# Joining layer 1 and layer 3 tiles on one load of the A weights

## The chip, the cores and the metric

The kernel runs on one core of one Trainium2 chip. The metric is the device time of one execution in microseconds (us); the median of 12 runs of the kernel before is 2137.83 us (2132.86 to 2146.22). A core has a matrix engine (TensorE, PE in the profile; its weight loads are PEld), VectorE (DVE), ScalarE (ACT), GpSimd (POOL) and SyncE (SP), which here only issues transfers. Matmul results go to PSUM[...]; all other tiles lie in SBUF.

## The reference, cut to what matters

Four layers run over a sequence of 2048 positions with 576 features, each with a layernorm ahead of it and a residual sum behind it: A, B, A, B.

```python
x = A_x
x = x + _A_ref(_layernorm(x), A_wqkv, A_wo)                       # layer 1
x = x + _B_ref(_layernorm(x), B_mem0, B_Wq, B_Wk, B_Wv, B_Wo, 32) # layer 2
x = x + _A_ref(_layernorm(x), A_wqkv, A_wo)                       # layer 3
x = x + _B_ref(_layernorm(x), B_mem0, B_Wq, B_Wk, B_Wv, B_Wo, 32) # layer 4
```

A is a local attention: 32 heads of 18 features; each position attends to itself and to seven earlier positions, two apart, so a tile needs 14 positions (a halo) of the tile ahead of it. Its weights are `wqkv` (576 by 1728) and `wo` (576 by 576), and layers 1 and 3 use the same ones. B goes through the sequence in 64 segments of 32 positions, with 32 heads of 128 features and eight memory rows; the memory rows that come out of one segment go into the next, so B is a chain of 64 steps in each layer.

## The kernel before, in words

Activations are kept transposed, features on the partitions (576 = 4 x 128 + 64, so five chunks) and positions in the columns. A works on tiles of T = 64 positions (32 tiles in a layer), B on segments of 32.

**B** is done for layers 2 and 4 at once: in step t, lane 0 is segment t of layer 2 and lane 1 is segment t - 5 of layer 4 (`DLY` = 5), 69 steps in all. One step (`b_step`) has eleven groups of Q and K projections (`qk`, lines 832 and 835, 80 moving columns for both lanes), the V projections (`vpass`, line 879), two halves of scores and softmax (lines 919 to 929, then DVE, ACT, POOL), two halves of weighted sums (`pv`, line 970) and the output projection (`oproj`, line 994). Its weights stay in SBUF.

**A** is done by `a_tile(layer, j, ...)`, once for each of 64 (layer, tile) pairs. It does the layernorm (two PE sums at line 470, `stats` on DVE, `rstd` on ACT, `wr` on POOL), then Q, K and V: for each of the three parts, five output blocks `c` of 128 features, each the sum of five matmuls with 64 moving columns (line 570), then an evacuation `ev` for the part. The blocks start at the features `CB` = 0, 126, 252, 378, 448, so that no head is cut. Then come the products q times k on POOL, the logits on PE (line 619), a softmax, the spreading of the weights (line 644), the products with v on DVE, three adds, and the output projection (line 680, five blocks of five matmuls of 64 columns), the residual sum (line 686) and a second layernorm whose result, `xnb1` or `xnb3`, is B's input.

A's weights do not stay in SBUF. `wload` brings them in strips of up to 256 output features (`[128, 5*256]`, 320 KB, or 160 KB for a strip of 128): three strips for each of Q, K, V and three for the output, twelve for a tile. The very first tile takes them into the room of B's output weights; the next two gather them from the inputs (lines 503 and 504) into a ring of three buffers (`ring`), and the third writes each strip out to a contiguous copy (line 513); from then on they are fetched from that copy (line 507). Each load sits on SP's queue and waits until a ring buffer comes free. Layer 3's tile j is started when lane 0 has finished segments 2j and 2j+1; layer 1's tile j five steps ahead of its use (`LEAD`).

**The order of the work** is written out ahead of the run by a planner (`_Plan.run`). Every operation has a cost, a priority, the buffers that it takes and those that it gives back; the planner goes through time and gives each engine its next ready operation. What comes out is one fixed list of instructions for each engine, which the chip executes in that order. The planner has a cost for changing the matmul form (`SWITCH`, 0.097 us; forms F, C and R), and a model of PE's instructions arriving in pages of 256 (`PAGE`, `FETCH`). The dictionary `PR` holds the priorities.

Of the kernel before, what the change touches and what calls it, by code (L numbers as in the profile page):

```python
# [34 lines left out]
HPC = 7  # L35
EPS = 1e-5
NQ = T // 16
CB = (0, 126, 252, 378, 448)
# [202 lines left out]
def _evac(n):  # L241
    return (_act(n), _dve(n))
# [4 lines left out]

class _K:
    def __init__(self, ctx, tc, A_x, A_wqkv, A_wo, B_mem0, B_Wq, B_Wk, B_Wv, B_Wo, out):
        self.ctx, self.tc, self.nc = ctx, tc, tc.nc  # L250
        self.A_x, self.A_wqkv, self.A_wo = A_x, A_wqkv, A_wo
        self.B_mem0, self.B_Wq, self.B_Wk, self.B_Wv, self.B_Wo = B_mem0, B_Wq, B_Wk, B_Wv, B_Wo
        self.out = out
        _, self.S, d = A_x.shape
        assert d == D and self.S % P == 0
        assert B_Wq.shape[1] == NH and B_Wq.shape[2] == P and B_mem0.shape[1] == NM
        self.NT = self.S // T
        self.NSEG = self.S // SEG
        self.dly = DLY
        self.nsteps = self.NSEG + self.dly  # L260
        self.scale_b = float(P) ** -0.5
        self.pl = _Plan()
        self.halo = {}
# [22 lines left out]
    def setup(self):  # L286
# [8 lines left out]
        self.strips = [dp.tile([P, 5 * 256], BF16, name=f"strip{i}") for i in range(12)]  # L295
# [11 lines left out]
        for t_, pat, b0 in ((epad[:, 0:4, :], [[CB[1], 4]], 0), (epad[:, 4, :], [], CB[4])):  # L307
            self.sel(t_, pat + [[-AD, AH]], 1, b0, ALU.is_ge, 0.0)
            self.sel(t_, [[-a, n] for a, n in pat] + [[AD, AH]], -1, AD - 1 - b0, ALU.is_ge, 0.0)
        self.sel(epad[:, 0:4, :], [[0, 4], [0, AH]], -1, HPC * AD - 1, ALU.is_ge, 0.0)  # L310
        self.sel(epad[:, 4, :], [[0, AH]], 1, CB[4] - 4 * HPC * AD, ALU.is_ge, 0.0)
# [3 lines left out]
        for t_, pat, b0 in ((et[:, 0:4, :], [[CB[1], 4]], 0), (et[:, 4, :], [], CB[4])):  # L315
            self.sel(t_, pat + [[1, P]], -AD, b0, ALU.is_ge, 0.0)
            self.sel(t_, [[-a, n] for a, n in pat] + [[-1, P]], AD, AD - 1 - b0, ALU.is_ge, 0.0)
        nc.gpsimd.memset(et[:, 0:4, HPC * AD:P], 0.0)
        nc.gpsimd.memset(et[:, 4, 0:4 * HPC * AD - CB[4]], 0.0)
# [36 lines left out]
        tiles("qk", 7, [P, 3, 2, W80])  # L356
# [3 lines left out]
        tiles("x1", 2, [P, 5, T], F32)  # L360
        tiles("x3", 2, [P, 5, T], F32)
# [4 lines left out]
        tiles("xn", 1, [P, 5, T])  # L366
        tiles("qT", 1, [P, 5, T])
        tiles("kT", 1, [P, 5, HALO + T])
        tiles("vT", 2, [P, 5, HALO + T])
# [6 lines left out]
        tiles("oT", 1, [P, 5, T])  # L376
# [3 lines left out]
        tiles("ring", 3, [P, 5 * 256])  # L380
# [10 lines left out]
        st = wo[64:128, 0:9 * 1280].rearrange("p (a b) -> p a b", b=1280).rearrange("p (a c) b -> p a c b", c=3)  # L391
        nc.vector.memset(st[:, :, 0:2, 1024:1280], 0.0)
        nc.vector.memset(st[:, :, 2, 512:640], 0.0)
        nc.vector.memset(wo[:, 11 * 1280:12 * 1280], 0.0)
        nc.vector.memset(mem0T[:], 0.0)
        for t_ in self.pl.pools["ring"]:
            nc.vector.memset(t_[64:128, :], 0.0)
# [91 lines left out]
    def wload(self, i, src, rows, col0, n, prio, dep):  # L489

        pl, dma = self.pl, self.nc.sync.dma_start
        step, last = rows
        self.strip_n[i] = k = self.strip_n.get(i, -1) + 1
        w = pl.buf("ring") if k else None

# [3 lines left out]
        def gather(e):  # L501
            f, v, r, m = src[0:1, col0:col0 + 1], view(), min(P, src.shape[0] - last), min(n, src.shape[1] - col0)
            dma(out=v[:, 0:4, 0:m], in_=bass.AP(f.tensor, f.offset, [[src.shape[1], P], [step * src.shape[1], 4], [1, m]]))
            (dma if k else self.nc.scalar.dma_start)(out=v[0:r, 4, 0:m], in_=src[last:last + r, col0:col0 + m])

        def fetch(e):
            dma(out=w.t[:, 0:5 * n], in_=self.strips[i][:, 0:5 * n])
        if k == 0:
            o = self.first = pl.op("SP", 0.65, gather, -20.0 + 0.01 * i, lat=4.0)
            return view, (), o  # L510
        o = pl.op("SP", 0.9 if k <= COPY else 0.5, gather if k <= COPY else fetch, prio, [dep, self.strip_in.get(i)], acq=[w], lat=4.0)
# [4 lines left out]
    def a_tile(self, layer, j, dep, due, span):  # L516

        nc, pl = self.nc, self.pl
        first = j == 0
        early = layer == 1 and j < 2  # L520
# [3 lines left out]
        Q = PR[f"A{layer}"]  # L524
        if layer == 1:
            xT = pl.buf("x1")
            x0, ps = pl.buf("x0"), pl.buf("r")
            a = pl.op("SP", 0.5, lambda e: nc.sync.dma_start(out=x0.t[0:T, 0:D], in_=self.A_x[0, j * T:(j + 1) * T, :]),
                      pr(0) if j else -30.0, [dep, self.first if j else None], acq=[x0])

            def tr(e, ps=ps):
                for c in range(5):
                    nc.tensor.matmul(ps.t[:, c * T:(c + 1) * T], lhsT=x0.t[:, c * P:(c + 1) * P], rhs=self.ident[:, 0:T],
                                     start=True, stop=True)
            b = pl.op("PE", 0.16, tr, pr(0.04), [a], acq=[ps, xT], uses=[x0], mm=5)
            o_x = pl.op(AD_, _evac(320), lambda e, ps=ps: self.copy(e, xT.t[:], ps.t[:, 0:5 * T].rearrange("p (c t) -> p c t", c=5)),
                        pr(0.05), [b], uses=[ps, xT])
        else:
            xT = self.acc[0][j][0]
            o_x = self.x_done[0][NS * j + NS - 1]  # L540

        xn = pl.buf("xn")

        def wr(e, m, rstd):
            x4, o4, xt, ot = xT.t[:, 0:4], xn.t[:, 0:4], xT.t[0:64, 4], xn.t[0:64, 4]
            self.tt(e, o4, x4, m.unsqueeze(1).to_broadcast([P, 4, T]), ALU.subtract)
            self.tt(e, ot, xt, m[0:64], ALU.subtract)
            self.tt(e, o4, o4, rstd.unsqueeze(1).to_broadcast([P, 4, T]), ALU.mult)
            self.tt(e, ot, ot, rstd[0:64], ALU.mult)
        gate = pl.op("NONE", 0.0, None, pr(Q[0]), [o_x], acq=[xn])  # L550

        wgate = pl.op("NONE", 0.0, None, pr(Q[0]), [gate, self.x1_stored[0]]) if layer == 1 and j == 1 else gate
        o_n = self.layernorm(xT, gate, pr(Q[0]), wr, 2.4, wuses=[xn], early=early)

        dst = {0: pl.buf("qT"), 1: pl.buf("kT"), 2: pl.buf("vT")}
        qT, kT, vT = dst[0], dst[1], dst[2]
        hin = self.halo.get(layer)
        got = {}
        for part in (0, 1, 2):
            ps = pl.buf("r")  # L560
            o = o_n
            for c in range(5):
                if c % 2 == 0:
                    n = 256 if c < 4 else P
                    view, w, ow = self.wload(part * 3 + c // 2, self.A_wqkv, (P, 512), part * D + CB[c], n, pr(Q[1]) - PR[f"ring{layer}"], wgate)
                w0 = c % 2 * CB[1]

                def mm(e, c=c, view=view, ps=ps, w0=w0):
                    for kc in range(5):
                        nc.tensor.matmul(ps.t[:, c * T:(c + 1) * T], lhsT=view()[:, kc, w0:w0 + P], rhs=xn.t[:, kc, :],  # L570
                                         start=(kc == 0), stop=(kc == 4))
                o = pl.op("PE", 0.146, mm, pr(Q[1] + 0.03 * part), [o, ow], acq=[ps, dst[part]] if c == 0 else (),
                          uses=[xn, *w] if c == 0 else [xn, *w, ps], lat=0.0 if c < 4 else None, mm=5)
                if c == 0 and part > 0:
                    def hcopy(e, part=part):
                        h = dst[part].t[:, :, 0:HALO]
                        if first:
                            nc.vector.memset(h, 0.0)
                        else:
                            self.copy(e, h, hin[0].t[:, part - 1])  # L580
                    got[part, "h"] = pl.op("DVE" if first else ("POOL", "ACT") if early else "POOL", 0.25, hcopy, pr(Q[1]), [o] if first else [o, hin[1]],
                                           uses=[dst[part]] if first else [dst[part], hin[0]])

            def ev(e, part=part, ps=ps):
                i = ps.t[:, 0:5 * T].rearrange("p (c t) -> p c t", c=5)
                if part == 0:
                    self.copy(e, qT.t[:], i, scale=float(AD) ** -0.5)
                else:
                    self.copy(e, dst[part].t[:, :, HALO:HALO + T], i)
            got[part] = pl.op(AD_, _evac(320), ev, pr(Q[1] + 0.02 + 0.03 * part), [o], uses=[ps, dst[part]])  # L590
        if j + 1 < self.NT:
            hk = pl.buf(f"halo{layer}")

            def hsave(e):
                self.copy(e, hk.t[:, 0], kT.t[:, :, T:T + HALO])
                self.copy(e, hk.t[:, 1], vT.t[:, :, T:T + HALO])
# [565 lines left out]
```

## Time and profile before

| what | value |
|---|---|
| median of 12 runs | 2137.83 us |
| the profiled execution, its own time | 2137.7 us |
| its span, first to last instruction | 2136.0 us |
| PE busy | 2016.7 us, 94%, 60717 matmuls |
| DVE, ACT, POOL busy | 1416.3, 1138.3, 833.0 us |
| bytes moved by DMA | 265.14 MB, mean 124 GB/s |
| A's QKV matmuls, line 570 | 4800 (75 of them on the first tile) |
| A's output matmuls, line 680 | 1600 (25 of them on the first tile) |

The profile is of one execution. A line such as `L570 PE MATMUL r<-xn,ring` is a group of instructions: line of the kernel, engine, operation, the tile written and the tiles read. "Idle before" is time in which the engine had nothing running ahead of that instruction, with what ended it; `issue` means that nothing that the profile shows was being waited for. A matmul is recorded with some 200 ns from its first read to its end, while the next one starts much sooner; the pace of the engine is read from the start times.

### The profile page before, as it was taken

Reading aid. Unit: us, or ns where it says so; the run is one execution under the profiler, and the core shown is the slowest. Engines: PE = TensorE matmul, PEld = TensorE weight load, DVE = VectorE, ACT = ScalarE, POOL = GpSimd, SP = SyncE. Lnnn points to the kernel's source line nnn. Section 1 sums busy time; section 2 is a strip of 40 time slices with the busy share of each in tenths; the row PEclk is TensorE's granted clock in tenths of the full one; section 3 lists DMA queues with packets and bytes.
Section 4 is the critical chain, followed back from the end, with each engine's and each line's share of the span. In section 5 each row is a group of like instructions: output and inputs, shape, how many; then the busy total and the mean of one; then the engine's idle time right before and its main releaser. Section 6 shows DMA issues by size and latency. Waiting matters only on the chain.

```text
span 2136.0 us, 132983 instructions
## 1 busy us (share of the span) xinstructions
PE 2016.7 (94%) x60717; PEld 1732.3 (81%) x60717; DVE 1416.3 (66%) x3754; ACT 1138.3 (53%) x2803; POOL 833.0 (39%) x1289
## 2 busy tenths in 40 slices
PE   1699999999999999999999999999999999999998
PEld 1577888888888888888888888888888888888876
DVE  4477676766666666666766676667667666665565
ACT  1355565555555555555555555556555555655554
POOL 2244434444343344434434443443444434342220
PEclk7899999999999999999999999999999999999999
DMA  9744343343343344334433433344334333341220
GB/s 324 201 152 136 122 126 123 124 141 105 125 127 123 112 124 141 108 122 126 126 120 114 140 121 112 123 127 127 123 124 132 112 116 121 125 122 58 76 76 10
DMA packets 158307, 265.14 MB, mean 124 GB/s; under 512 B 23464, under 2 KB 89904, under 8 KB 157616
## 3 DMA queue, kind: packets, MB, share of 16 engines
q1 hardware_dynamic: 152016, 237.38, 35.7%
q0 software_dynamic: 4576, 18.88, 2.5%
q8 instruction: 474, 7.77, 1.5%
q14 instruction: 89, 0.73, 0.1%
q10 hardware_dynamic: 1152, 0.39, 0.1%
HBM read 240.46 MB, written 16.12 MB: 120 GB/s over the span
## 4 chain that ended last, share of the span: by engine, by line
PE 90%; DMA 6%; issue 2%; DVE 2%; ACT 0%; SPq 0%; ACTq 0%; DVEq 0%
PE r L832 28%; PE r L994 18%; PE r L879 17%; PE r L570 7%; PE r L835 6%; PE r L970 3%; DMA ring<-strip 3%; PE r L680 2%; PE r L470 2%; PE r L644 2%; PE r L929 1%; PE r L919 1%; DMA x<-in_B_mem_dram 1%; PE r L619 1%; PE r L923 1%
## 5 line engine op out<-in xcount | busy, mean ns | idle before, releaser
L832 PE MATMUL r<-hT,wk 128*128 128x80 bf16 (+1 forms) x8832 | 662.9, 199 | 2.2 <-issue 2.2
L832 PE MATMUL r<-hT,wq 128*128 128x80 bf16 (+1 forms) x8832 | 660.7, 198 | 3.7 <-ACT hT L276 2.7
L832 PEld LDWEIGHTS <-wq 128*128 128x128 bf16 x8832 | 501.1, 99 | 46.6 <-issue 34.0
L835 PE MATMUL r<-hT,wqk_r 128*128 128x160 bf16 (+1 forms) x2208 | 507.2, 230 | 0.0
L276 ACT ACTIVATE qk<-r 128x480 bf16<-128x480 f32 (+2 forms) x668 | 351.6, 527 | 265.3 <-PE r L835 254.2
L994 PE MATMUL r<-OT,wo 128*128 128x80 bf16 (+1 forms) x11040 | 418.6, 200 | 33.4 <-issue 28.9
L832 PEld LDWEIGHTS <-wk 128*128 128x128 bf16 x8832 | 447.3, 99 | 1.8 <-issue 1.8
L994 PEld LDWEIGHTS <-wo 128*128 128x128 bf16 x11040 | 395.1, 100 | 44.8 <-issue 40.4
L879 PE MATMUL r<-wv,hT 128*32 128x512 bf16 x5376 | 355.2, 381 | 1.7 <-issue 1.4
L283 POOL TENSOR_TENSOR big<-qT,kT 128x1024 bf16<-128x1024 bf16 x189 | 314.8, 1687 | 58.5 <-ACT kT L276 32.4
L283 POOL TENSOR_TENSOR ex<-ex,sum 128x320 bf16<-128x320 bf16 x138 | 107.0, 775 | 567.7 <-DVE sum L779 495.6
L879 PEld LDWEIGHTS <-hT 128*32 128x32 bf16 x6720 | 172.2, 96 | 127.8 <-issue 3.8
L276 ACT ACTIVATE V<-r 128x512 bf16<-128x512 f32 x305 | 181.4, 596 | 158.1 <-PE r L879 158.0
L835 PEld LDWEIGHTS <-wqk_r 128*128 128x128 bf16 x2208 | 219.7, 99 | 1.0 <-issue 1.0
L768 DVE TENSOR_REDUCE nmx<-r 128x8 f32<-128x320 f32 x276 | 133.2, 483 | 107.7 <-PE r L923 107.5
L276 ACT ACTIVATE OT<-r 128x320 bf16<-128x320 f32 (+1 forms) x378 | 134.3, 422 | 112.9 <-PE r L970 112.6
L570 PE MATMUL r<-xn,ring 128*128 128x64 bf16 x4725 | 176.6, 194 | 15.4 <-DMA ring<-in_A_wqkv_dram 10.2
L570 PEld LDWEIGHTS <-ring 128*128 128x128 bf16 x4725 | 157.2, 98 | 34.2 <-issue 15.1
L276 ACT ACTIVATE big<-r 128x256 bf16<-128x256 f32 (+1 forms) x288 | 109.0, 430 | 91.5 <-PE r L644 90.6
L1013 DVE CAST hT<-r 128x64 bf16<-128x64 f32 (+1 forms) x68 | 14.9, 219 | 200.9 <-PE r L994 200.8
L283 POOL TENSOR_TENSOR xnb<-x,st 128x256 bf16<-128x256 f32 x124 | 64.6, 521 | 208.8 <-DVE st L476 208.8
L769 DVE TENSOR_TENSOR r<-r,nmx 128x320 f32<-128x320 f32 x276 | 137.7, 499 | 9.5
(147 smaller groups left out, 2978.4 us busy)
## 6 DMA issues: line engine op xcount, KB each, us to landing
ring<-strip SPq DMA_DIRECT2D x488, 320.0 KB, 3.4
ring<-strip SPq DMA_DIRECT2D x244, 160.0 KB, 4.0
x1T<-x SPq DMA_DIRECT2D x32, 160.0 KB, 4.1
x<-x1T SPq DMA_DIRECT2D x32, 160.0 KB, 4.1
x3T<-x SPq DMA_DIRECT2D x32, 160.0 KB, 4.8
x<-x3T SPq DMA_DIRECT2D x32, 160.0 KB, 4.6
wo<-in_B_Wo_dram POOLq DMA_DIRECT2D x4, 1152.0 KB, 24.5
wq<-in_B_Wq_dram POOLq DMA_DIRECT2D x2, 2048.0 KB, 20.7
```

The costliest lines, as they stand in the source:

```text
L276: nc.scalar.activation(out=out, in_=in_, func=ACT.Copy, scale=1.0 if scale is None else scale)
L283: (self.nc.vector if e == "DVE" else self.nc.gpsimd).tensor_tensor(out=out, in0=in0, in1=in1, op=op)
L470: nc.tensor.matmul(psf, lhsT=(self.ones if c < 4 else self.ones_h)[:, :], rhs=xs.t[:, c].rearrange("p a t -> p (a t)"), start=(c == 0), st ...
L570: nc.tensor.matmul(ps.t[:, c * T:(c + 1) * T], lhsT=view()[:, kc, w0:w0 + P], rhs=xn.t[:, kc, :], start=(kc == 0), stop=(kc == 4))
L644: nc.tensor.matmul(ps[g].t[:, c * P:(c + 1) * P], lhsT=self.epadT[q4, c0 + c, :], rhs=e_.t[q4].rearrange("p w t -> p (w t)"), start=True, ...
L768: nc.vector.tensor_reduce(out=m, in_=v, axis=AX.X, op=ALU.max, negate=True)
L769: nc.vector.tensor_tensor(out=v, in0=v, in1=m.unsqueeze(len(shp) - 1).to_broadcast(shp), op=ALU.add)
L832: nc.tensor.matmul(pv[:, hh, wi, a:b], lhsT=self.Wb[wi][0][:, kc, h * P:(h + 1) * P], rhs=hT.t[:, kc, a:b], start=(hh == 0 and wi == 0 and ...
L835: nc.tensor.matmul(pv[:, hh, :, a:b], lhsT=self.Wb[0][1][:, h * P:(h + 1) * P], rhs=hT.t[:, 4:6, a:b], start=False, stop=(hh == n - 1), sk ...
L879: nc.tensor.matmul(ps.t[c * 32:(c + 1) * 32, :], lhsT=l, rhs=w, start=(kc == 0), stop=(kc == 4))
L970: nc.tensor.matmul(ps[c].t[:, i * n + a - c0:i * n + z - c0], lhsT=V[b].t[q4, r, i, :], rhs=pt.t[q4, i, b, a:z], start=(i == 0 and b == bl ...
L994: nc.tensor.matmul(psY.t[:, mb * W80 + c0:mb * W80 + c1], lhsT=self.wo[:, w0:w0 + P], rhs=self.OT[:, h % 16 // 4 * 8 + h // 16 * 4 + h % 4 ...
```

## The change

`a_tile` now takes a list `parts` of one or two (layer, tile) pairs. With two, layer 1's tile lies in columns 0 to 63 and layer 3's in columns 64 to 127 of `xn`, `qT`, `kT`, `vT`, and each QKV matmul has 128 moving columns. The features are cut at multiples of 128 (`CB` and `HPC` go, the masks `epad` and `epadT` follow), and the last 64 features of Q, K and V share one strip and two blocks, so there are seven strips and 14 blocks for a QKV round and three strips for an output round. The attention itself (`a_attend`) is still done tile by tile, layer 3 first.

The output projection is `a_out`. From layer 1's tile 6 on (`EXTRA` = 3), layer 1's attention result is held in `oT` (`self.pend`) and its output is done one round later, together with that of the next layer 3 tile, with 128 moving columns.

The rounds are: layer 1's tiles 0, 1, 2 alone; then for layer 3's tile j = 0 to 27 a pair with the next layer 1 tile, with layer 1's tile 6 alone ahead of j = 3; then layer 3's tiles 28 to 31 alone.

Buffers: `ring` 3 to 2, `qk` 7 to 6, `x1` 2 to 3, `vT` 2 to 1 (of twice the size), `xn`, `qT`, `kT`, `oT` twice the size. The residual sum of a tile becomes two DVE instructions. `PR` gets new values, and for each of them one for the first 12 steps (`_e`) and one for the last 8 (`_l`), which `_at(t)` picks.

```diff
-    def wload(self, i, src, rows, col0, n, prio, dep):
+    def wload(self, i, prio, dep):
...
+        n = P if i == 9 else 256
...
+        if i < 6:
+            cols = ((i // 2 * D + i % 2 * 256, 256),)
+        elif i == 6:
+            cols = ((512, 64), (D + 512, 64), (2 * D + 512, 64))
+        else:
+            cols = (((i - 7) * 256, 256 if i < 9 else 64),)
...
-    def a_tile(self, layer, j, dep, due, span):
+    def a_tile(self, parts, late_, dep):
...
-        for part in (0, 1, 2):
-            ps = pl.buf("r")
-            o = o_n
-            for c in range(5):
-                if c % 2 == 0:
-                    n = 256 if c < 4 else P
-                    view, w, ow = self.wload(part * 3 + c // 2, self.A_wqkv, (P, 512), part * D + CB[c], n, pr(Q[1]) - PR[f"ring{layer}"], wgate)
-                w0 = c % 2 * CB[1]
-
-                def mm(e, c=c, view=view, ps=ps, w0=w0):
-                    for kc in range(5):
-                        nc.tensor.matmul(ps.t[:, c * T:(c + 1) * T], lhsT=view()[:, kc, w0:w0 + P], rhs=xn.t[:, kc, :],
-                                         start=(kc == 0), stop=(kc == 4))
...
+        for b in range(14):
+            part, c = (b // 4, b % 4) if b < 12 else (3, b - 12)
+            i, w0 = (b // 2, b % 2 * P) if b < 12 else (6, (b - 12) * P)
+            if i not in strips:
+                strips[i] = self.wload(i, pr(Q[1]) - p["ring1"], wgate)
...
+            def mm(e, c=c, view=view, ps=ps, w0=w0):
+                for kc in range(5):
+                    nc.tensor.matmul(ps.t[:, c * n:(c + 1) * n], lhsT=view()[:, kc, w0:w0 + P], rhs=xn.t[:, kc, 0:n],
+                                     start=(kc == 0), stop=(kc == 4))
...
+            late = layer == 1 and late_
+            if layer == 3 and pend is not None:
+                oT, o_go = pend[4:6]
+            else:
+                oT = pl.buf("oT")
+                o_go = pl.op("NONE", 0.0, None, pr(Q[0]), [gates[0], dep], acq=[oT])
+            o_o, o_l = self.a_attend(layer, j, l, layer // 2, dst, oT, got, o_go, dep, pr, p[f"A{layer}"], early)
...
+    def a_out(self, jt, parts, o_l, pr, p, Q, early):
...
         for mb in range(5):
             if mb % 2 == 0:
-                n = 256 if mb < 4 else P
-                view, w, ow = self.wload(9 + mb // 2, self.A_wo, (CB[1], CB[4]), mb * P, n, pr(Q[6]) - PR[f"ring{layer}"], o_l)
+                view, w, ow = self.wload(7 + mb // 2, pr(Q[6]) - p["ring3"], o_l)
             w0 = mb % 2 * P
...
                 for c in range(5):
-                    nc.tensor.matmul(ps.t[:, mb * T:(mb + 1) * T], lhsT=view()[:, c, w0:w0 + P], rhs=oT.t[:, c, :], start=(c == 0), stop=(c == 4))
...
+                    nc.tensor.matmul(out, lhsT=view()[:, c, w0:w0 + P], rhs=oT.t[:, c, s0:s0 + n], start=(c == 0), stop=(c == 4))
...
+            def add(e, xT=xT, l=l):
+                v = ps.t[:, 0:4 * n].rearrange("p (c t) -> p c t", c=4)[:, :, l * T:(l + 1) * T]
+                nc.vector.tensor_tensor(out=xT.t[:, 0:4], in0=xT.t[:, 0:4], in1=v, op=ALU.add)
+                nc.vector.tensor_tensor(out=xT.t[0:64, 4], in0=xT.t[0:64, 4], in1=ps4.t[0:64, l * T:(l + 1) * T], op=ALU.add)
...
+        its, n1 = [([(1, j)], False) for j in range(3)], 3
+        for j in range(NT):
+            if j == EXTRA:
+                its.append(([(1, n1)], True))
+                n1 += 1
+            its.append((([(1, n1)] if n1 < NT else []) + [(3, j)], j >= EXTRA and n1 < NT))
+            n1 += 1
...
+            while nl < len(its) and t >= (NS * its[nl][0][-1][1] + NS if its[nl][0][-1][0] == 3 else NS * its[nl][0][0][1] - LEAD):
+                self.a_tile(*its[nl], self.qk_op.get(t - 1))
                 nl += 1
...
+X1 = 3
+X3 = 2
+OTB = 1
+QKB = 6
+RING = 2
```

## The prediction

> **What bounds the kernel now.** I read the page's first part, then the table of stretches, then PE's waits in the steady part, then PE's instructions in order of time.
>
> ```profile
> PE 2016.7 (94%) x60717; PEld 1732.3 (81%) x60717; DVE 1416.3 (66%) x3754; ACT 1138.3 (53%) x2803; POOL 833.0 (39%) x1289
> 200.00:2000.00 1800.00, 1764.49 (x52478) 1523.23 (x52475) 1212.43 (x3198) 993.45 (x2401) 739.38 (x1145) 1.00 0.39 121
> ```
>
> The second line is the stretch from 200 to 2000 us: PE, PEld, DVE, ACT, POOL. PE is idle for 35.5 of 1800 us at full clock. The other 84 us of its idle time lie in the first 200 us (70 us, B's weights arriving) and at the end (14 us). So for nine tenths of the run the end is set by how long PE's list takes, and the list's idle time has one main cause:
>
> ```profile
> PE r L994 <- issue: 27.1, 37, 2.1
> PE r L970 <- issue: 2.4, 4, 0.8
> PE r L570 <- DMA ring<-strip: 1.3, 4, 0.4
> PE r L680 <- DMA ring<-strip: 1.1, 3, 0.6
> ```
>
> These are PE's waits in that stretch (total us, times, longest). Late strips cost 2.4 us. "Issue", a wait for nothing that the profile shows, costs 31.2 us with its smaller rows (0.9, 0.5, 0.3). The order of time shows what it is:
>
> ```profile
> 723.64 0.42 PE L994 MATMUL r<-OT,wo 128*128 128x80 bf16 x7 [0.35 <-issue]
> 723.90 0.31 PE L680 MATMUL r<-oT,ring 128*128 128x64 bf16 x5
> 724.15 0.54 PE L970 MATMUL r<-pt,V 32*128 32x48 bf16 x48
> 724.62 2.61 PE L994 MATMUL r<-OT,wo 128*128 128x80 bf16 x68
> 729.31 1.32 PE L994 MATMUL r<-OT,wo 128*128 128x80 bf16 x32 [2.08 <-issue]
> ```
>
> Between two such stops lie 7 + 5 + 48 + 68 = 128 matmuls, with their weight loads 256 instructions. The page's instruction queue says the same: 474 packets and 7.77 MB are 16.4 KB each, and 2 x 60717 / 256 = 474. PE stands at the border of an instruction page that has not come. The 128 matmuls ran in about 3.4 us; over the whole run a page has 2136 / 474 = 4.5 us. At the stop at 666.66 us (1.79 us long) the engines that carry the page were full: of the DMA view's forty slices of 662 to 668 us the first sixteen read 9999989999899875, and in them lay a ring strip of 5.2 us from issue to landing and the store of x1.
>
> **What the Trainium skill says.** "Runtime: NRT & Kernel Launch", section "Instruction fetch mechanics": instructions come in blocks of 256, fetched while the current one runs, "mostly hidden". The trace agrees on 256 and disagrees on hidden: 31 us. "DMA: Bandwidth & Descriptors", section "Queues, rings and completion order": each DMA engine takes its queues in turn, a packet at a time, so a page shares its engine with the strips; the 662 us stop agrees. "TensorE: Matmul & The Clock Gate", section "Wait — 56ns, not 53.3ns?": a warm matmul takes its columns at 2.4 GHz plus about 2.5 ns, so 29.2 ns for 64 columns and 55.8 for 128. The trace has both:
>
> ```profile
> 1117.95 0.89 PE L570 MATMUL r<-xn,ring 128*128 128x64 bf16 x25
> 1118.68 0.31 PE L533 MATMUL r<-ident,x 128*128 128x64 bf16 x5
> ...
> 1011.89 0.39 PE L470 MATMUL r<-xs,ones 128*128 128x128 bf16 x4
> 1012.11 0.22 PE L470 MATMUL r<-xs,ones_h 128*128 128x128 bf16 x1
> 1012.17 0.31 PE L832 MATMUL r<-hT,wq 128*128 128x80 bf16 x4
> ```
>
> By starts, 25 matmuls of 64 columns take 0.73 us, 29.2 ns each; five of 128 take 0.28 us, 56 ns each. Weight loads do not set the pace even at 64 columns, so sharing a load gains little by itself: the columns stay.
>
> **The change part by part.**
>
> *Matmuls.* Before: 64 tiles x (75 + 25) = 6400 x 29.2 ns = 186.9 us. After, by the list of rounds: 28 pairs and 8 single tiles for QKV, at 70 matmuls; output in 26 pairs and 12 singles (tiles 0 to 5 of layer 1, 0 to 2 and 29 to 31 of layer 3), at 25. In pairs 28 x 70 + 26 x 25 = 2610 x 56 = 146.2 us; single 8 x 70 + 12 x 25 = 860 x 29.2 = 25.1 us; together 171.3. **Saved on PE: 15.6 us**, two thirds of it from 14 blocks in place of 15. It lies on PE's list, so all of it counts.
>
> *Instruction pages.* 2930 matmuls fewer, so 57787, 451 pages, 4.7 us each in the same span. A page with 25 of A's matmuls had 0.73 us of them, and now 1.4 us. Most of the stops I looked at have such a block in the page that stops or in the one before (25 of line 680 in the five lines above). And strip loads fall from 64 x 12 = 768 to 36 x 7 + 38 x 3 = 366, in bytes from about 200 MB (488 x 320 KB + 244 x 160 KB) to 104 (33 x 7 + 35 x 2 = 301 large, 35 small). So the pages have more time and less beside them. The stops cost 31.2 us as idle time; by starts somewhat more, because the last matmul's record runs some 0.17 us into each of about 46: some 39 us. The trace of before can't show the remainder. Bounds: a gain of 39 us (none left), or a loss of about 10 (the new order puts two dense pages together more often). I take two fifths, **16 us**.
>
> *Late strips.* 2.4 us in the steady part, half as many loads, a ring of two in place of three: a gain of **1 us**; the other end is the rival below.
>
> *Other engines, at nothing.* The residual sum goes from 0.487 us (its row at line 686) to about 0.62 (a 128x256 float32 row on DVE is 0.416, a 64x64 one 0.206): 64 x 0.13 = 8 us on DVE, which has a third of its time free. The evacuations of Q, K, V go from six of 0.438 us to three of 512 columns (V's row: 0.596) and three small ones (0.25 to 0.30), 2.6 us both ways. POOL's products, halo copies and layernorm writers keep their number. If that cover were gone, PE would wait for an evacuation; in the steady part only 1.0 us of PE's waits name DVE, and none ACT or POOL. SP issues 400 loads fewer; in the first three rounds strip 6 takes six issues of 0.4 to 0.5 us in place of two, about 5 us over three rounds, in time when SP waits for ring buffers.
>
> *Fewer buffers.* Six `qk` buffers are just those that one half of the scores reads, so the seventh group can't start before the scores of the first half: PE needs about 1 us of other work there, twice in a step, and has V passes and A's blocks for it. One `oT` holds layer 1's result until the next round; the round that ends it is started four steps ahead of its use (tile j + 4 is finished in the round of step 2j + 4 and used from step 2j + 8). Layer 3's tile now waits for both layernorms and for 14 blocks, a few us more, of three steps of 31 us that it has. Counted at nothing.
>
> *Order.* The whole list is new. A change of matmul form costs about 0.1 us (25 matmuls of line 570 took 0.83 us at 1028.47, ahead of a V pass, against 0.73) and there are some 15 in a step, so one in ten more or fewer is 10 us. I take 0 and keep 10 both ways; start and end likewise 0, with 5 both ways.
>
> *Sum.* 2137.7 (the profiled execution, span 2136.0 and 1.7 around it; the median is 0.1 away) - 15.6 - 16 - 1 = **2105 us**, faster by 1.5%.
>
> **The rivals.**
>
> *Only the columns.* The page stops stay, because they sit in line 994 and `pv`, which are unchanged (27.1 of 31.2 us): 2137.7 - 15.6 - 1 = 2121. For it: those two alone fill 128 matmuls in 3.4 us. Against: the bytes beside the pages halve.
>
> *Everything goes.* All 39 us of stops and 5 of the start: 2137.7 - 15.6 - 39 - 5 = 2078. Against: `pv` and line 994 stay dense.
>
> *The ring of two becomes the bound.* A strip is used up in 10 x 56 ns = 0.56 us, and fetching the next one takes 3.4 us to land, with issue and wait about 4; two buffers give seven strips in about 14 us. PE's list can't step round a late strip. 366 loads: from 33 / 366 = 0.09 us of lateness on the average strip the gain is gone. If two in five are late by 0.4 us (a late one cost 2.4 / 7 = 0.34 so far), 146 x 0.4 = 58 us: 2105 + 58 = 2163, slower. For it: SP's longest waits are for ring buffers (687.8 us behind line 570). Against: a round has 61 us for ten strips, and less traffic makes each faster.
>
> *The change does not do what it says:* 128 columns cost more than two times 64. The line 470 rows exclude it.
>
> **How the numbers follow.** What I forecast (2090 to 2116) 0.52; everything goes (under 2090) 0.13; only the columns (2116 to 2133) 0.21; small losses of order eat the gain (within 0.2%, about what this kernel's measurement can tell, 2133.5 to 2142) 0.05; the ring or another new wait (above 2142) 0.09. Leaving out some 0.1 at each end: 2078 to 2137. Faster 0.86, same 0.05, slower 0.09; the likeliest case's own range is 2090 to 2116.
>
> **What would show it.** 57787 matmuls; PE's busy time near 2000 us; 451 or 452 instruction packets; some 170 MB moved; L994's "issue" at 13 to 20 us. Right for the wrong reason: the matmuls as counted, but issue unchanged and the gain in the first 200 us. Wrong: waits for ring strips above 15 us, a new wait of L832 for `qk` evacuations, or of `hT` for `xnb3` (layer 3 late).

## The result, and the profile after

The changed kernel takes 2128.64 us (median of 12 runs, 2122.87 to 2132.60) against 2139.61 for the kernel before (49 runs): a ratio of 0.9947, 95% interval 0.9934 to 0.9960. It is faster, by 0.5% and not by 1.5%. The profiled executions have spans of 2128.2 and 2136.0 us.

The page of the changed kernel, its busy times, packets and bytes:

```profile
PE 2004.9 (94%) x57787; PEld 1720.8 (81%) x57787; DVE 1425.0 (67%) x3839; ACT 1168.9 (55%) x2869; POOL 809.1 (38%) x1219
DMA packets 100392, 168.14 MB, mean 79 GB/s; under 512 B 16904, under 2 KB 55824, under 8 KB 99728
```

Matmuls, instruction packets (451) and bytes are what the prediction counted. PE's busy time fell by 11.8 us. PE's waits between 200 and 2000 us (total us, times, longest) have changed accordingly; these are rows of the kernel after:

```profile
PE r L570 <- DMA ring<-strip: 3.6, 4, 1.4
PE r L908 <- ACT hT L280: 3.6, 3, 1.6
...
PE r L747 <- DMA ring<-strip: 2.6, 2, 1.6
...
PE r L1070 <- issue: 1.7, 4, 0.9
PE r L570 <- issue: 0.8, 1, 0.8
```

The page stops, 31.2 us before, are down to 2.5 us. Late strips cost 6.2 us, up from 2.4, and waits for `hT` (3.6 us) and `oT` (2.2 us) are new.

To see when time was won and lost, I take the starts of B's steps 0, 12 and 60 in both traces: the step's first matmul with `wqk_r`, line 835 before and 911 after. From PE's instructions in order of time (start, duration, line, tiles), before:

```profile
57.98 0.23 PE L835 MATMUL r<-hT,wqk_r 128*128 128x80 bf16 x1
422.49 0.23 PE L835 MATMUL r<-hT,wqk_r 128*128 128x160 bf16 x1
1909.11 0.23 PE L835 MATMUL r<-hT,wqk_r 128*128 128x160 bf16 x1
```

and after:

```profile
71.27 0.23 PE L911 MATMUL r<-hT,wqk_r 128*128 128x80 bf16 x1
462.64 0.23 PE L911 MATMUL r<-hT,wqk_r 128*128 128x160 bf16 x1
1899.28 0.23 PE L911 MATMUL r<-hT,wqk_r 128*128 128x160 bf16 x1
```

| stretch | before, us | after, us | difference |
|---|---|---|---|
| start to step 0 | 58.0 | 71.3 | +13.3 |
| steps 0 to 12 | 364.5 | 391.4 | +26.9 |
| steps 12 to 60 | 1486.6 | 1436.6 | -50.0 |
| step 60 to the end | 226.9 | 228.9 | +2.0 |
| sum (the spans) | 2136.0 | 2128.2 | -7.8 |

So the change is worth about 50 us where the pipeline is full, more than the whole forecast, and 40 of these are lost before step 12. The table of stretches shows for steps 0 to 12 and 12 to 60 how much of it PE was busy (PE, PEld, DVE, ACT, POOL busy with their instructions, the granted PE clock, the share of DMA, GB/s), before:

```profile
57.98:422.49 364.51, 337.21 (x10417) 285.58 (x10414) 248.16 (x656) 188.50 (x488) 147.97 (x217) 0.98 0.46 141
422.49:1909.11 1486.62, 1456.28 (x43340) 1257.74 (x43337) 1010.20 (x2662) 822.33 (x1994) 616.98 (x956) 1.00 0.39 123
```

and after:

```profile
71.27:462.64 391.37, 350.20 (x10052) 293.20 (x10049) 249.83 (x672) 198.81 (x512) 149.28 (x210) 0.94 0.32 93
462.64:1899.28 1436.64, 1431.85 (x40809) 1238.26 (x40806) 1010.93 (x2708) 843.14 (x2031) 591.36 (x897) 1.00 0.24 69
```

In steps 12 to 60 PE's idle time falls from 30.3 to 4.8 us, and its busy time by 24.4 us. In steps 0 to 12 the idle time rises by 13.9 us, from 27.3 to 41.2, and the busy time by 13.0 us; the lower mean clock there, 0.94 and not 0.98, has a part in that.

The experiments take the two halves one after the other. Each is compared with the kernel before. Each trace shows one execution: a second trace of the changed kernel has step 12 at 465.1 us and not at 462.6, so a few us of difference at one step tell nothing.

### The profile page after: what moved, and what is told of

It reads as the page before. It is cut to its first block, busy times and chain, and to the rows that moved or that the text cites. A ratio compares the mean times of both kernels' runs of the same rounds, so it can differ in the third digit from the quotient of the medians.

```text
span 2128.2 us, 126521 instructions
## 1 busy us (share of the span) xinstructions
PE 2004.9 (94%) x57787; PEld 1720.8 (81%) x57787; DVE 1425.0 (67%) x3839; ACT 1168.9 (55%) x2869; POOL 809.1 (38%) x1219
## 5 line engine op out<-in xcount | busy, mean ns | idle before, releaser
L280 ACT ACTIVATE qk<-r 128x480 bf16<-128x480 f32 (+2 forms) x688 | 364.7, 530 | 297.7 <-PE r L911 287.1
L287 POOL TENSOR_TENSOR big<-qT,kT 128x512 bf16<-128x512 bf16 x187 | 314.0, 1687 | 129.1 <-DVE oT L287 76.5
L955 PEld LDWEIGHTS <-hT 128*32 128x32 bf16 x6720 | 162.6, 96 | 139.9 <-POOL hT L282 4.3
L280 ACT ACTIVATE V<-r 128x512 bf16<-128x512 f32 x281 | 167.5, 598 | 107.8 <-PE r L955 107.5
L280 ACT ACTIVATE OT<-r 128x320 bf16<-128x320 f32 (+1 forms) x401 | 145.6, 426 | 107.9 <-PE r L1046 107.6
L280 ACT ACTIVATE big<-r 128x384 bf16<-128x384 f32 (+1 forms) x316 | 117.9, 437 | 136.7 <-PE r L703 131.0
L287 POOL TENSOR_TENSOR xn<-x,st 128x256 bf16<-128x256 f32 x124 | 75.5, 630 | 272.3 <-DVE st L475 159.2
L570 PE MATMUL r<-xn,ring 128*128 128x128 bf16 (+1 forms) x2450 | 164.9, 215 | 12.8 <-DMA ring<-in_A_wqkv_dram 8.2
L570 PEld LDWEIGHTS <-ring 128*128 128x128 bf16 x2450 | 133.3, 98 | 21.4 <-DMA ring<-in_A_wqkv_dram 9.1
L955 PE MATMUL r<-wv_r,hT 128*32 128x512 bf16 x1344 | 132.8, 381 | 0.0
```

What stands on the lines that cost most here:

```text
L280: nc.scalar.activation(out=out, in_=in_, func=ACT.Copy, scale=1.0 if scale is None else scale)
L287: (self.nc.vector if e == "DVE" else self.nc.gpsimd).tensor_tensor(out=out, in0=in0, in1=in1, op=op)
L570: nc.tensor.matmul(ps.t[:, c * n:(c + 1) * n], lhsT=view()[:, kc, w0:w0 + P], rhs=xn.t[:, kc, 0:n], start=(kc == 0), stop=(kc == 4))
L955: nc.tensor.matmul(ps.t[c * 32:(c + 1) * 32, :], lhsT=l, rhs=w, start=(kc == 0), stop=(kc == 4))
```

## Experiments on the steady part: why 50 us and not 33

**Giving the matmuls back.** The changed kernel in the same order, but each 128-column matmul of a pair is two of 64 (the cut shows QKV; `a_out` is done alike):

```diff
-                    nc.tensor.matmul(... rhs=xn.t[:, kc, 0:n])
+                    for h in range(m):
+                        nc.tensor.matmul(... rhs=xn.t[:, kc, h * T:(h + 1) * T])
```

> The kernel after, with the same written order, but each of the 2610 matmuls of 128 columns in a pair done as two of 64 columns, so 60397 matmuls and 472 instruction pages; strip traffic as after (168 MB). More work on PE: 2610 x 2.6 ns = 7 us. Theory density (fewer and longer matmuls took the page stops away): PE's issue waits between 200 and 2000 us come back from 2.5 us to about 25, and the time is about 2128.6 + 7 + 23 = 2159. Rival traffic (less beside the pages took them away) and rival order (the new list keeps the dense stretches apart): issue stays below 6 us and the time is about 2136.

Measured: 2145.92 us, ratio 1.0035 (1.0022 to 1.0048); 60397 matmuls, 472 instruction packets. Steps 12 to 60 take 16.8 us more than in the changed kernel. PE's idle time there is 12.2 us and not 4.8, nearly all of the difference "issue". The other 9.5 us are busy time; by the prediction's rates the split costs 2 x 29.2 - 56 = 2.4 ns for each of 24 x 95 pairs in these steps, 5.5 us. Part of the remaining 4 us is stops too, since the record of the last matmul runs into a stop, as the prediction says. Between 200 and 2000 us "issue" waits come back to 9.1 us (6.7 in `wo`'s matmuls, 1.7 in `pv`, 0.7 in A's), without any more traffic. That lies between what density and what its rivals would have given (25, or below 6): density is a part of the cause and not the whole.

**Giving the traffic back.** The changed kernel in the same order, but behind each strip's load the strip is also copied to a spare place in DRAM that nobody reads, so that strips move twice:

```diff
             dma(out=w.t..., in_=self.strips[i]...)
+            dma(out=self.dup[self.ndup % 16][:, 0:5 * n], in_=self.strips[i][:, 0:5 * n])
```

> The kernel after, with the same written order; every strip fetch is followed by a second transfer of the same strip into a spare place in DRAM that nothing reads, so the strips move some 210 MB in place of 104, about what the kernel before moved. Theory traffic: issue waits of PE between 200 and 2000 us rise from 2.5 us to 15 or more, and the time to 2145 or more. Theory density and rival order: issue stays below 6 us; late strips may cost a few us, 2129 to 2136.

Measured: 2164.16 us, ratio 1.0123 (1.0078 to 1.0168), with 272.55 MB moved (265.14 in the kernel before, though in 158307 packets, where this kernel has 115067). Steps 12 to 60 take 17.8 us more. PE's waits between 200 and 2000 us in this kernel show both effects of the traffic, pages that come late and strips that come late (14.6 us in all, just short of the 15 expected, and 11.3). The largest row of each:

```profile
PE r L1049 <- issue: 8.6, 15, 1.4
PE r L573 <- DMA ring<-strip: 6.2, 8, 1.5
```

Only the pages belong to the steady part: in steps 12 to 60 "issue" takes 12.0 us (1.5 in the changed kernel) and late strips 0.2; the other late strips lie ahead of step 12.

**Taking traffic from the kernel before.** The kernel before, same order and same 60717 matmuls, but each load of a strip brings only 64 of its 128 partitions. The other half of each strip is left out, so this kernel does not compute what the others do:

```diff
-            dma(out=w.t[:, 0:5 * n], in_=self.strips[i][:, 0:5 * n])
+            dma(out=w.t[0:64, 0:5 * n], in_=self.strips[i][0:64, 0:5 * n])
```

> The kernel before, with the same written order; each fetch of a strip from its copy brings 64 of 128 partitions only, so half the bytes (about 165 MB in all) and a wrong part of A's weights. Theory traffic: issue waits of PE between 200 and 2000 us fall from 31.2 us to 12 or less, and the time to about 2115. Theory density and rival order: issue stays at 25 to 31 us, time 2130 to 2138.

Measured: 2095.01 us, ratio 0.9800 (0.9771 to 0.9830), with 165.20 MB and 474 instruction packets; 20 us less than the expectation for the traffic gave. Not one matmul is gone, and 2% of the time is. The only row of "issue" left between 200 and 2000 us:

```profile
PE r L994 <- issue: 5.0, 12, 1.0
```

27.1 us of L994 and 31.2 us in all have become 5.0, and no late strip shows in that stretch. Steps 12 to 60 take 1452.0 us, 34.6 fewer. That is what fewer bytes beside the pages are worth there, late strips (1.7 us) included. PE's idle time in these steps is 4.8 us, as in the changed kernel, so the bytes alone, in the old order, take away as much idle time as the whole change did. Packets fell with the bytes, to 111459, so this run does not part the two. From 1452.0 the changed kernel gets to 1436.6: another 15.4 us, all of it busy time, of which the columns explain 24 x (200 x 29.2 - 95 x 56) ns = 12.5; the remaining 2.9 us stay open.

**Both together.** The matmuls split and the strips moved twice:

> The kernel after, same written order, with both: matmuls of a pair as two of 64 columns (472 pages) and every strip moved twice (some 210 MB of strips). If density and traffic explain all of the page stops that the change took away, PE's issue waits between 200 and 2000 us come back to about 31 us, and the time is about 2128.6 + 17 + 35, less what both runs share, 2175 to 2195. If the order of the list has a part of its own, issue stays at about 20 us, some 7 from density and 13 from traffic added up, and the time is near 2175.

Measured: 2202.16 us, ratio 1.0266 (1.0219 to 1.0313), above the span expected. "Issue" waits between 200 and 2000 us add up to 43.8 us, above both sums expected, with these two largest rows:

```profile
PE r L1076 <- issue: 18.4, 25, 1.5
PE r L1052 <- issue: 15.7, 22, 1.7
```

2.5 us in the changed kernel, 9.1 with the matmuls back, 14.6 with the traffic back, 43.8 with both: the two together cost more than their sum. That fits a race between the time that PE takes for a page and the time that the next page takes to come, which no run measures by itself. With both undone the new order stops no less than the old one did (31.2), though the traffic given back has other packets and comes in pairs of transfers. A cleaner pair says the same: the split kernel and the kernel before with half of its strips have nearly the same bytes (168.48 and 165.20 MB) and matmuls, and differ in their order; they stop for 9.1 and 5.0 us. So nothing shows that the order itself helps; it was the bytes, and next to them the matmuls.

## Experiments on the start: where 40 us went

**Start to step 0, +13.3 us.** The first tile's layernorm was late: ACT wrote its `xs` 18 us later. In the kernel before, ACT issued one more transfer of a strip's last rows and went on (start, duration, engine, line; in brackets the idle time before and what ended it):

```profile
9.51 0.47 ACT L464 ACTIVATE xs<-x 128x320 bf16<-128x320 f32 x1 [0.54 <-issue]
```

After the change it had to issue strip 6's last rows first, now three transfers (the last 64 features of Q, K and V share the strip), and stood in that issue for 13.77 us:

```profile
13.86 13.77 ACTq L509 DMA_DIRECT2D wo<-in_A_wqkv_dram  x3
27.68 0.47 ACT L463 ACTIVATE xs<-x 128x320 bf16<-128x320 f32 x1 [17.25 <-DMA wo<-in_A_wqkv_dram]
```

ACT stood in such issues in the kernel before too (4.58 us for two of them at 11.14 us, 5.85 for two at 23.45), but only behind the writing of `xs`.

What filled the DMA engines was B's weights. Their loads are issued by POOL behind the set-up of the masks, and the masks had become cheaper: ten selects for `epad` and `epadT` were now four. POOL's first weight load, before:

```profile
7.90 0.72 POOL L420 DMA_DIRECT2D wqk_r<-in_B_Wq_dram  x1 [0.17 <-issue]
```

and after:

```profile
6.36 0.72 POOL L419 DMA_DIRECT2D wqk_r<-in_B_Wq_dram  x1 [0.24 <-issue]
```

The DMA view of 4 to 12 us (packets, MB, share of the 16 engines; q1 carries the part of A's strips that SP issues, q0 B's weights) before:

```profile
q1 hardware_dynamic: 4186, 1.71, 86.0%
q0 software_dynamic: 42, 0.34, 17.6%
```

and after:

```profile
q1 hardware_dynamic: 3188, 1.39, 71.3%
q0 software_dynamic: 79, 0.57, 36.4%
```

A thousand of the strips' small packets (mean 1.71 MB / 4186 = 0.4 KB) didn't get through, since weights with packets of 7 to 8 KB (0.57 MB / 79) came 1.5 us sooner and took the engines' time. The Trainium skill ("DMA: Bandwidth & Descriptors", section "Queues, rings and completion order") says that an engine serves its queues in turn, a packet at a time, a packet being a bundle of typically 9 to 17 descriptors. If what the profile counts is served in turn like that, the queue with small packets loses in bytes; these rows agree, but no run here tries the size of packets by itself. To test the time of issue, the weights are made to wait again. Eight more selects of a mask (each gives the same mask once more) stand ahead of POOL's loads:

```diff
+        for _ in range(8):
+            self.sel(mx[:, 1, NM:KL], [[-1, SEG]], 1, 0, ALU.is_ge, NEG)
```

> The kernel after, with eight more mask instructions of about 0.19 us on POOL ahead of its issues of B's weights, so that these start some 1.5 us later, near where they started before (7.90 us in place of 6.36). Theory of the start: the first tile's strips are small packets that share the DMA engines with B's weights one packet against one, so each us that the weights start sooner costs the strips many us; the first K and Q group then starts at about 60 us in place of 71, and the time is about 2118. Rival (the 64-column pieces of strip 6, or the order on ACT, are slow by themselves): the first group stays at 69 to 73 us and the time at 2127 to 2130.

Measured: 2117.92 us, ratio 0.9899 (0.9869 to 0.9928). More work on POOL, and the kernel is faster. The weights were issued at 8.78 us and not 6.36, ACT passed its three issues in 2.02 us, and step 0 started 15.8 us sooner:

```profile
10.94 2.02 ACTq L511 DMA_DIRECT2D wo<-in_A_wqkv_dram  x3
...
55.43 0.23 PE L913 MATMUL r<-hT,wqk_r 128*128 128x80 bf16 x1
```

The lead is kept to the end: the span is 2110.9 us, 17.3 shorter than the changed kernel's (the profiled execution is the fastest of four; by the medians the gain is 10.7 us). The hold is 0.9 us longer than one that would restore the old time of issue (7.90 us), and that strip 6 now takes three such transfers of ACT, ahead of `xs`, was not tried by itself, so the share of these three in the 13.77 us stays open; that the weights' time of issue decides whether they are slow is shown. More of the same, 32 selects, with the weights issued at 15.63 us:

> The kernel after with 32 mask instructions in place of eight, so B's weights start some 6 us later. Theory (one packet of the strips against one of the weights): by then nearly all of the first tile's strips have been taken, the first tile is done sooner still, and the first K and Q group waits for B's weights, 50 to 55 us; time 2112 to 2118, no more than a few us better than with eight. Rival (the 1.5 us happened to be the right time): later than with eight, 2120 or more.

Measured: 2121.58 us, ratio 0.9909 (0.9894 to 0.9924). Step 0 starts still sooner, at 46.4 us (50 to 55 expected), but step 1 at 101.7, which with eight selects was 98.4. The gain of 9 us has become a loss of 3.4 within one step. Between the two steps PE waits for the strips of A's next tile, longer than with eight selects (13.0 us):

```profile
PE r L572 <- DMA ring<-in_A_wqkv_dram: 23.1, 6, 12.6
```

These strips now meet B's later weights: from 46.4 to 73 us q0 has 91.6% of the engines' time, and from 55.4 to 72 us with eight selects 69.4%. That fits a hold that only moves the collision to the next tile; a longer one than eight selects gave no more. The same 32 selects in the kernel before ask whether that kernel too had something to win there:

> The kernel before with the same 32 mask instructions ahead of B's weights (start at about 14 us in place of 7.90). If the mechanism is general, its first group starts somewhat sooner than 58.0 us or about there, and the time is 2130 to 2138; if the weights' arrival bounds its start, all moves by 6 us and the time is 2140 to 2146.

Measured: 2143.02 us, ratio 1.0015 (0.9999 to 1.0031), within what can be told from no change. Step 0 is 14 us sooner, step 1 3.3 us later and step 12 5 us later. The kernel before had no loss there whose recovery lasts.

**Steps 0 to 12, +26.9 us.** By the same starts, steps 6, 9 and 10 take 39.0, 41.4 and 39.1 us, and in the kernel before 29.3, 32.4 and 29.5: 28.3 us more, as much as the whole loss. (Step 1 takes 9.0 us more; steps 0, 3, 4 and 5 take that back.) These three steps in the table of stretches of the kernel after, and then three windows of 3.4 us at the end of step 6:

```profile
249.00:288.00 39.00, 31.47 (x882) 27.25 (x879) 28.56 (x71) 18.73 (x48) 17.27 (x23) 0.91 0.23 67
352.00:394.00 42.00, 37.49 (x936) 32.13 (x934) 21.50 (x62) 20.93 (x51) 18.96 (x26) 0.92 0.36 106
394.00:433.00 39.00, 34.31 (x921) 29.27 (x918) 27.98 (x76) 21.64 (x54) 18.27 (x26) 0.91 0.20 62
```

```profile
277.50:280.90 3.40, 1.34 (x32) 0.82 (x28) 3.16 (x8) 1.45 (x4) 0.00 (x0) 0.99 0.52 139
280.90:284.30 3.40, 1.65 (x25) 1.68 (x25) 1.54 (x6) 0.83 (x2) 0.87 (x2) 0.50 0.56 180
284.30:287.70 3.40, 0.74 (x11) 0.53 (x10) 0.85 (x4) 1.46 (x5) 2.45 (x7) 0.50 0.79 206
```

PE is idle for 17 of 120 us in these steps, and its clock is not full. In 277 to 288 us PE has next to nothing that it may do, and what it waits for is the outputs of two tiles, layer 3's and then layer 1's, each still done by itself, 64 columns at a time:

```profile
280.14 0.32 PE L747 MATMUL r<-oT,ring 128*128 128x64 bf16 x5 [1.57 <-DMA ring<-strip]
282.65 0.69 PE L747 MATMUL r<-oT,ring 128*128 128x64 bf16 x10 [2.19 <-POOL oT L287]
```

Step 6 is in the rounds ahead of `EXTRA`, in which layer 3's tiles are already joined with layer 1's in QKV while their outputs are not; the last of these single outputs ends at 372 us, in step 9. Step 10 has joined work alone. Two causes were possible: buffers (the ring of two, six `qk`), or the list that the planner wrote for these rounds. Eleven of the planner's priorities (ten of the first steps, and `qk` of the middle of the run), `EARLY` and `EXTRA` were set otherwise. The buffers are those of the change; with `EXTRA` at 0 all of layer 3's outputs but the last three are joined:

```diff
+PR.update(qk=(0.307, -0.732), qk_e=(32.672, -2.164), qkd_e=(0.044, 0.537), s0_e=(-31.468, 1.847), p0_e=(-42.77, 3.192),
+          p1_e=(-0.493, 0.433), od_e=(-6.266, -15.728), ring1_e=12.854, ring3_e=8.188, asp_e=0.199, a1_e=4.215)
-EARLY = 12
+EARLY = 4
-EXTRA = 3
+EXTRA = 0
```

> The kernel after with another written order of the first rounds: the extra layer 1 tile goes ahead of the first pair (EXTRA 3 to 0), so that every round is a full pair with a joint output from the start, the priorities for the first steps hold for 4 steps in place of 12, and eleven of them have other values. The ring of two, the six qk buffers and the joint rounds stay. Theory order (the 27 us lost between steps 0 and 12 were written into the order of the first rounds): step 12 starts some 20 us earlier than the 462.5 us of the kernel after, the first group of step 0 still at 71 us, and the time is about 2107. Rival buffers (a ring of two and six qk buffers cost those 27 us, whatever the order): step 12 stays within 5 us of 462.5, time 2124 to 2130.

Measured: 2107.66 us, ratio 0.9846 (0.9832 to 0.9861). Step 0 is as late as in the changed kernel (72.2 us), step 12 is 22.5 us sooner. Its start, and the sum of the same three stretches as above:

```profile
440.15 0.23 PE L911 MATMUL r<-hT,wqk_r 128*128 128x160 bf16 x1
...
sum 120.00, PE 119.70 PEld 103.59 DVE 84.80 ACT 72.88 POOL 47.06; mean PE 39.90 PEld 34.53 DVE 28.27 ACT 24.29 POOL 15.69
```

In the three stretches PE is busy for 119.7 of 120 us, and no late strip is left between 200 and 2000 us. With the same two ring buffers and six `qk` buffers, so it was the list. The kernel with both remedies:

> The order of the run before, and the eight mask instructions on POOL ahead of B's weights. If both losses at the start are separate, the gains add: 2128.6 - 10.7 - 21 = about 2097, with step 0 at 56 us and step 12 at about 425. If the new order only used the time in which PE waited for B's weights anyway, they do not add: about 2107.

Measured: 2096.54 us, ratio 0.9795 (0.9780 to 0.9809), the 2097 of two gains that add. It beats both kernels; its step 0 starts at 55.5 us and its step 12 at 424.2, where the kernel before had 57.98 and 422.49.

Of that list, one constant could be tried alone, with all priorities as in the change: `EXTRA` at 1, so that the joined outputs begin with layer 3's second tile.

> The changed kernel with one constant changed: EXTRA 1 in place of 3, so the joined outputs begin with layer 3's second tile and not with its fourth, and layer 1's extra tile comes ahead of j = 1. No planner cost is changed; the list that the planner writes has step 12 some 11 us sooner. If the loss between steps 0 and 12 lies in how the written list arranges the first rounds, and this list is as good on the chip as it is written, step 12 starts at 450 to 453 us (462.5 in the changed kernel, 440.1 with the other list) and the time is 2115 to 2121 us. If what matters is the planner's costs for the first twelve steps alone, and not where joining begins, step 12 stays at 460 to 466 us and the time at 2125 to 2132 us. Step 0 stays at 71 to 72 us in both.

Measured: 2116.88 us, ratio 0.9932 (0.9905 to 0.9959); step 12 at 447.7 us, 15 sooner than in the changed kernel, and the span 14.2 shorter. But the kernel before ran at 2131.38 us beside it, and the ratio's interval covers the changed kernel's ratio. So it was timed once more with the changed kernel beside it.

> The changed kernel itself, beside the kernel with EXTRA at 1 on the same chip, since that one's ratio to the kernel before did not part it from the changed kernel's. The ratio to the kernel before is 0.993 to 0.996, as it was.

> EXTRA at 1, once more beside the changed kernel. If the 14 to 15 us that its trace is ahead from step 12 to the end are worth their time, its median lies 11 to 16 us below that of the changed kernel in the same call (ratio to the kernel before about 0.987 to 0.990). If they are not, the two medians lie within 5 us.

Measured: the changed kernel 2127.97 us, ratio 0.9934 (0.9911 to 0.9957), with step 12 at 465.1; `EXTRA` at 1 2122.15 us, ratio 0.9911 (0.9884 to 0.9938), with step 12 at 454.6 and a span 11.4 us shorter. The medians lie 5.8 us apart, fewer than expected, and the intervals overlap. Where joining begins is part of the loss: 10 to 15 us of the traces, less of the medians. The traces also say where: with `EXTRA` at 1 steps 9 and 10 take 28.8 and 31 us again in both, step 6 stays at 39 to 40, and step 5 rises from 31.8 to 36.9 and 41.7. In step 5 the QKV of layer 1's single tile now ends; in the changed kernel it ends in step 9. How much of the loss that tile holds, and which of the eleven priorities hold the remainder, is not settled.

## Why the prediction was wrong, point by point

The direction was right and the time lay in the range, but the gain was a third of the forecast, and it came out of two errors of opposite sign.

- **Order, start and end: the step that failed.** "I take 0 and keep 10 both ways; start and end likewise 0, with 5 both ways." They cost 40 us before step 12 and 2 after step 60. Two things were passed over. The diff took six selects from POOL's set-up, and the prediction spoke of POOL's products and writers but did not follow POOL's queue, in which the weight loads stand behind these selects: 13.3 us, and 15.8 came back when they were held again. And it priced the new list by changes of matmul form, a cost of the steady part, although the diff gives the first twelve steps their own priorities and leaves layer 3's first outputs unjoined, so that they are the place where the list is new: 26.9 us, of which another list gave 22.5 back by step 12.
- **Instruction pages: right mechanism, wrong size.** Forecast 16 us, measured 34.6 in steps 12 to 60 with late strips included, when only the bytes fell. The bound of 39 was near it. For two fifths no reason of its own was given; against more stood that L994 and `pv` stay dense, and the third experiment shows that density alone stops little (5.0 us). That the trace "disagrees on hidden" was also too strong: 46 stops between 200 and 2000 us stand against some 410 pages (2 x 52478 / 256), so nine borders in ten showed none.
- **Matmuls, 15.6 us: right.** 57787 of them, and 12.5 us in 24 rounds fit what lies between the third experiment and the changed kernel (15.4). The share of the 14 blocks was put at two thirds; 320 x 29.2 ns = 9.3 us is three fifths.
- **Late strips: wrong in sign, small.** 6.2 us, not 1.4. They lie in the first rounds and are gone with another list.
- **Fewer buffers and other engines, at nothing: right in the steady part.** With the same buffers the other list leaves PE idle for 3.9 us in steps 12 to 60, and the changed kernel for 4.8.
- **The rivals.** The time of 2128.64 us fell into the case "only the columns" (2116 to 2133), for another reason: the stops went, as in "everything goes", and the start took the gain. That it lay in the range was luck. The ring of two did not become the bound: 6.2 us of waits, not above 15. The checks on matmuls, packets and bytes could not have told this; L994's "issue" could, at 1.7 us where 13 to 20 was written. Of the signs of being wrong, a wait for `hT` came, of 3.6 us.

Left open are the last stretch, 2 us longer, in which PE now waits 3.3 us for `xs` and 2.1 for `fin` (before: none and 0.4), which was not tried, and the split of the first rounds' loss.

## What to carry to other kernels

When a change shortens an engine's set-up, ask which transfers that engine issues behind it and whose queue they will fill: here weight loads issued 1.5 us sooner went with a first step 13 us later, and a hold of 2.4 us took that back. Price the fill of the pipeline apart from its steady part, and compare starts of equal steps in both traces before anything else; a small difference of spans can be two large ones. And where "issue" shows at the border of instruction pages, count the bytes moving beside them, not only the instructions.

## What the runs showed of the hardware that was not expected

- Page stops depend on density and traffic together: 2.5, 9.1, 14.6 and 43.8 us with neither, either and both given back. With half the bytes of its strips, a list of the same density lost 5.0 us and not 31.2.
- An engine that issues transfers can stand in the issue for 13.77 us; the same three issues took 2.02 us when the large packets of another queue came 2.4 us later.
- PE's clock fell to half at 280.9 us, when PE had been busy for 1.34 of the 3.4 us before and its longest wait there was 1.57 us: no single long wait was needed. The Trainium skill ("TensorE: Matmul & The Clock Gate", section "What's actually happening") puts the half rate after an idle window of about 3.4 us. In this trace a window with that much work in it was enough.
